# Sigmoid attention and an MLP mixer on one core: which unit transposes which tile, and a bias given as a number

## The chip, the cores and the metric

One core of a Trainium2 chip runs the whole program. The metric is the device time of one execution in microseconds (us), as the median of several runs. Kernels that are compared were run on the same chip in the same session. A ratio of two kernels is the mean time of one kernel's fast runs over the mean time of the other's fast runs of the same rounds, with a 95% interval, so it is not quite the ratio of the medians quoted beside it. Where I turn a ratio into microseconds, I multiply one minus the ratio by the median of the kernel before in that session.

TensorE is called PE in the profile (PEld is its weight load), VectorE DVE, ScalarE ACT, GpSimd POOL and SyncE SP. SP only issues DMA transfers here. The granted clock is the share of its full clock that PE was allowed at a time: 1.00 is full speed, 0.50 half.

## The reference, cut to what matters

```python
def _attn_ref(q, k, v):                       # 8 batches, 12 heads, 448 tokens, 64 wide
    scores = scale * q @ k.T - np.log(S)      # scale = 1/8, S = 448
    attn = 1.0 / (1.0 + np.exp(-scores))      # a sigmoid, no sum over a row
    return attn @ v

def _moe_ref(x, w_tok1, w_tok2, w_ch1, w_ch2):
    xt = x.transpose(0, 2, 1)                 # x: 8 x 448 x 768
    h = np.maximum(xt @ w_tok1, 0.0) @ w_tok2
    u = x + h.transpose(0, 2, 1)              # the "sums"
    h2 = np.maximum(u @ w_ch1, 0.0) @ w_ch2
    return u + h2
```

## The kernel before

The eight batches are four groups of two. A group has six head pairs, and each pair goes through scores (seven tiles `qk`, each followed by one sigmoid on ACT) and values. Then come the token mixing (`k` and `yn` in the profile), the sums u, and the channel mixing: 12 units of ch1 over token tiles 0 to 3, 12 over tiles 4 to 6, and 14 halves of ch2. While the channel mixing of one group runs (a "phase"), the attention of the next group is woven between its units, three rounds at a time. So group 0's attention stands alone at the start, and three mixed phases and one lone channel mixing follow.

Three things have to be transposed: k and q of each pair, the attention's result, and the sums. Cuts are marked `# ...`.

```python
def turn(n, whats=("k", "q")):                # k and q of head pair n (six per group)
    for what in whats:
        # ...
        if n >= NP:                           # groups 1 to 3: permute on DVE, transpose by DMA
            perm = pa.tile([128, J, 2, E], FP16, tag="perm", bufs=3, ...)
            nc.vector.tensor_copy(out=perm..., in_=raw[:, :, :, :])
            nc.sync.dma_start_transpose(out=t..., in_=perm...)
            continue
        ps = bank(f"t{what}_{n}", [128, J, 2, P], FP16)   # group 0: 14 transposes on PE; two PSUM buffers
        # ...
        nc.vector.tensor_copy(out=t[:, :, :, :], in_=ps[:, :, :, :])

def scores(self, i, j):                       # four matmuls into PSUM, then
    nc.scalar.activation(out=at[:, :, :], in_=ps[:, :, 0:S], func=SIGMOID,
                         bias=bias_t[:, :], scale=att_scale)     # bias_t: a [128, 1] tile

def attention_round(grp, r):
    # ...
    if j == 3 and not grp.first:              # two pairs ahead
        turn(grp.g * NP + i + 2)
    grp.scores(i, j)

def uturn(self, j, d0=0, d1=6, eng=nc.scalar, nj=1):      # the sums, by PE, emptied by ACT
    # ... nc.tensor.transpose per 128x128 block, then one copy out of PSUM

# end of a phase: what goes behind the halves of ch2
fronts = {
    0: lambda: front1(0),
    2: lambda: front1(1),
    3: lambda: front2((0, 1)),
    4: lambda: front2((2, 3)),
    5: lambda: (nxt.uturn(0, nj=2), front2((4, 5))),
    6: lambda: (nxt.uturn(2, nj=2), front2((6,))),
    7: lambda: nxt.uturn(4, nj=2),
}
```

## Time and profile before

| What | Before |
|---|---|
| median of 4 runs (lowest to highest) | 404.81 us (403.67 to 406.28) |
| span of the profiled run, PE busy in it | 401.5 us, 371.5 us |
| longest wait of PE, at group 1's first score tile | 7.5 us |
| first channel matmul of group 0 to the fifth channel unit | 67.54 to 85.77 us: 18.23 us |
| first channel matmul of group 2 to that of group 3 | 254.51 to 342.18 us: 87.67 us |
| one sigmoid of 128x896 | 1007 ns |

The two stretches in the table are the yardsticks of the whole study. The first contains the wait and the slow clock after it. The second is one complete mixed phase with one boundary between groups. The prediction shows the waits, the windows and the timeline behind them. From the page, only two lines are added: the first row of busy time and the granted clock in 40 slices of 10 us each.

```profile
PE 371.5 (93%) x3474; PEld 196.9 (49%) x3474; DVE 170.1 (42%) x315; ACT 203.4 (51%) x218; POOL 93.3 (23%) x159
...
PEclk9999999779999999999999999999999999999999
```

The two digits 7 lie between 70 and 90 us. ACT is busy for half the span, which reads like an engine that cannot matter. That reading is tested below.

### The profile page before, as it was taken

The page shows a single profiled execution, that of the slowest core. Times are in us where ns is not written, and L with a number is a line of the kernel's source. Part 1 is how long each engine was busy: PE and PEld are TensorE (multiplying, and loading weights), DVE is VectorE, ACT ScalarE, POOL GpSimd, SP SyncE. Part 2 cuts the span into 40 slices and gives each one's busy share as a digit, 9 for nine tenths or more (in the row PEclk, how much of TensorE's full clock was granted, in tenths as well). Part 3 has the DMA queues.
Part 4 walks back from the last instruction along what each step waited for, and adds up shares of the span by engine and source line. Part 5 has one row for each costly group of instructions (what it writes and reads, how often), then busy time and mean ns, then how long its engine had stood idle before and what let it go on. Part 6 is the DMA issues. An engine that isn't in the chain of part 4 may idle for free.

```text
span 401.5 us, 8197 instructions
## 1 busy us (share of the span) xinstructions
PE 371.5 (93%) x3474; PEld 196.9 (49%) x3474; DVE 170.1 (42%) x315; ACT 203.4 (51%) x218; POOL 93.3 (23%) x159
## 2 busy tenths in 40 slices
PE   2888877299999999999999999999999999999995
PEld 1444545134555555544555556544555556546663
DVE  1358686134432218644341229444431148455222
ACT  1996842168777531487867521687768312200000
POOL 9788171633333300033343200000000000000000
PEclk9999999779999999999999999999999999999999
DMA  7999999999999961179999952125433221000122
GB/s 107 183 176 165 204 190 205 142 133 150 157 135 159 211 138 61 59 71 166 154 127 149 229 96 79 41 46 72 93 59 112 64 80 41 39 0 2 78 102 95
DMA packets 79284, 45.85 MB, mean 114 GB/s; under 512 B 53008, under 2 KB 75536, under 8 KB 79248
## 3 DMA queue, kind: packets, MB, share of 16 engines
q0 software_dynamic: 25104, 21.93, 39.9%
q1 hardware_dynamic: 54144, 23.41, 31.4%
q8 instruction: 27, 0.44, 0.5%
q14 instruction: 9, 0.07, 0.1%
HBM read 43.84 MB, written 11.01 MB: 137 GB/s over the span
## 4 chain that ended last, share of the span: by engine, by line
PE 83%; DMA 9%; POOL 4%; DVE 2%; issue 1%; POOLq 0%; DVEq 0%
DMA k_3_1236<-in_k_dram 3%; DMA qT_1232<-qp_1233 2%; DMA w_tok_s<-in_moe_w_tok_dram 2%; DMA k_2_95<-in_k_dram 1%; DMA k_5_353<-in_k_dram 1%; PE c_0_2_0_1315 L321 1%; PE c_0_3_0_1323 L321 1%; PE c_2_4_1_4591 L338 1%; PE c_2_2_1_4421 L338 1%; PE c_2_2_0_4393 L338 1%; PE c_2_1_1_4332 L338 1%; PE c_2_0_1_4261 L338 1%; PE c_1_2_1_3290 L338 1%; PE c_1_2_0_3262 L338 1%; PE c_1_1_1_3184 L338 1%
## 5 line engine op out<-in xcount | busy, mean ns | idle before, releaser
L321 PEld LDWEIGHTS <-w_ch_t 128*128 128x128 f16 x576 | 53.9, 99 | 58.4 <-issue 14.3
L338 PEld LDWEIGHTS <-h2aT_1249 128*128 128x128 f16 x168 | 15.5, 98 | 13.2 <-issue 3.8
L338 PEld LDWEIGHTS <-h2aT_2460 128*128 128x128 f16 x168 | 15.4, 98 | 13.2 <-issue 3.8
L338 PEld LDWEIGHTS <-h2aT_3652 128*128 128x128 f16 x168 | 15.4, 98 | 13.2 <-issue 3.8
L338 PEld LDWEIGHTS <-h2aT_4783 128*128 128x128 f16 x168 | 16.4, 98 | 10.9
L211 PEld LDWEIGHTS <-w_tok_t 64*128 64x128 f16 x252 | 12.1, 94 | 9.4 <-issue 3.0
L239 PEld LDWEIGHTS <-w_tok_n 128*64 128x64 f16 x224 | 11.4, 109 | 9.6 <-issue 4.8
L91 POOL DMA_DIRECT2D k_0_2661<-in_k_dram x2 | 1.2, 604 | 38.9 <-DVE qp_2528 L111 38.9
L148 PE MATMUL qk_0_0_1277<-qT_1232,kT_1228 64*64 64x448 f16 x4 | 0.6, 566 | 7.5 <-DMA qT_1232<-qp_1233 7.5
L311 ACT ACTIVATE uT_3338<-ut_0_0_3548 128x1536 f16<-128x1536 f16 x1 | 1.5, 1451 | 8.9 <-PE ut_0_0_3548 L301 8.9
L311 ACT ACTIVATE uT_2146<-ut_0_0_2356 128x1536 f16<-128x1536 f16 x1 | 1.5, 1451 | 8.9 <-PE ut_0_0_2356 L301 8.9
L311 ACT ACTIVATE uT_4469<-ut_0_0_4679 128x1536 f16<-128x1536 f16 x1 | 1.4, 1450 | 8.9 <-PE ut_0_0_4679 L301 8.9
L122 PE MATMUL tk_135<-ident,k_0_77 128*64 128x128 f16 x14 | 1.0, 310 | 5.2 <-DMA k_0_77<-in_k_dram 5.2
L148 PEld LDWEIGHTS <-kT_1228 64*64 64x64 f16 x28 | 0.9, 123 | 8.9 <-issue 4.6
L155 ACT ACTIVATE attn_0_0_169<-qk_0_0_168,att_bias 128x896 f16<-128x896 f32 x1 | 1.0, 1007 | 7.5 <-PE qk_0_0_168 L148 7.5
L155 ACT ACTIVATE attn_0_0_1278<-qk_0_0_1277,att_bias 128x896 f16<-128x896 f32 x1 | 1.0, 1007 | 7.4 <-PE qk_0_0_1277 L148 7.4
L330 DVE TENSOR_SCALAR h2aT_1249<-c_0_2_0_1315 128x512 f16<-128x512 f32 x1 | 0.7, 692 | 7.1 <-PE c_0_2_0_1315 L321 7.1
L222 ACT ACTIVATE h1T_118<-k_0_0_512_1142 128x512 f16<-128x512 f32 x1 | 0.6, 597 | 5.4 <-PE k_0_0_512_1142 L211 5.4
L122 PEld LDWEIGHTS <-k_0_77 128*64 128x64 f16 x14 | 0.7, 164 | 5.1 <-DMA k_0_77<-in_k_dram 5.1
L222 ACT ACTIVATE h1T_3337<-k_2_0_384_3428 128x768 f16<-128x768 f32 x1 | 0.8, 810 | 4.7 <-PE k_2_0_384_3428 L211 4.7
L91 POOL DMA_DIRECT2D k_4_1306<-in_k_dram x2 | 1.3, 658 | 7.8 <-DVE qp_1233 L111 7.4
L222 ACT ACTIVATE h1T_2145<-k_1_0_384_2236 128x768 f16<-128x768 f32 x1 | 0.8, 811 | 4.4 <-PE k_1_0_384_2236 L211 4.4
(1293 smaller groups left out, 980.2 us busy)
## 6 DMA issues: line engine op xcount, KB each, us to landing
w_ch_t<-in_moe_w_ch_dram POOLq DMA_DIRECT2D x6, 768.0 KB, 11.2
w_tok_t<-in_moe_w_tok_dram POOLq DMA_DIRECT2D x2, 224.0 KB, 6.4
out_dram<-u_0_120 SPq DMA_DIRECT2D x1, 384.0 KB, 4.8
out_dram<-u_1_122 SPq DMA_DIRECT2D x1, 384.0 KB, 4.1
out_dram<-u_2_124 SPq DMA_DIRECT2D x1, 384.0 KB, 5.8
out_dram<-u_3_126 SPq DMA_DIRECT2D x1, 384.0 KB, 2.3
out_dram<-u_4_128 SPq DMA_DIRECT2D x1, 384.0 KB, 2.3
out_dram<-u_5_130 SPq DMA_DIRECT2D x1, 384.0 KB, 2.7
```

What stands on the lines that cost most here:

```text
L91: nc.gpsimd.dma_start(out=t[64 * b : 64 * b + 64, :, :, :], in_=src[2 * g + b, 2 * i : 2 * i + 2].rearrange("h (p j) e -> p h j e", j=J),)
L122: nc.tensor.transpose(out=ps[64 * h : 64 * h + 64, j, :, :], in_=raw[:, h, j, :], identity=ident[:, :],)
L148: nc.tensor.matmul(out=ps[64 * b : 64 * b + 64, h, 0:S], lhsT=kT[64 * h : 64 * h + 64, j, b, :], rhs=qT[64 * h : 64 * h + 64, :, b, :], st ...
L155: nc.scalar.activation(out=at[:, :, :], in_=ps[:, :, 0:S], func=SIGMOID, bias=bias_t[:, :], scale=att_scale,)
L211: nc.tensor.matmul(out=ps[:, b, 0 : c1 - c0], lhsT=w_tok1_t[64 * b : 64 * b + 64, j, 128 * tcb : 128 * tcb + 128], rhs=self.x_nat[64 * b : ...
L222: eng.activation(out=dst, in_=src, func=RELU)
L239: nc.tensor.matmul(out=d[64 * b : 64 * b + 64, :], lhsT=w_tok2_n[:, tcb, j, :], rhs=self.h1T[:, b, tcb, c0 + w * m : c0 + w * m + w], star ...
L311: eng.activation(out=dst, in_=src, func=COPYF)
L321: nc.tensor.matmul(out=ps[:, :, :], lhsT=w_ch1_t[:, db, 128 * cb : 128 * cb + 128], rhs=self.uT[:, db, j0:j1, :], start=(db == 0), stop=(d ...
L330: eng.tensor_scalar(out=dst, in0=ps[:, :, :], scalar1=0.0, scalar2=None, op0=MAX)
L338: nc.tensor.matmul(out=ps[:, :], lhsT=self.h2aT[:, cb, j, :], rhs=w_ch2_t[:, cb, c], start=(cb == 0), stop=(cb == NCB - 1),)
```

## The change

It has three parts. First, pairs 0 and 1 of group 1 are transposed by PE during group 0, which takes away the wait at group 1's first score tile. The last two of these evictions go to ACT. Second, the sigmoid's bias is an immediate number in place of a tile. Third, the sums of groups 1 to 3 are transposed by DMA, so that PE has 42 transposes fewer per group.

```diff
-    bias_t = pc.tile([128, 1], FP32, name="att_bias")
-    def turn(n, whats=("k", "q")):
+    def turn(n, whats=("k", "q"), eng=nc.vector):
-            if n >= NP:
+            if n >= NP + 2:
# ... the eviction goes to DVE or ACT as eng says
-                bias=bias_t[:, :],
+                bias=att_bias,
         def uturn(self, j, d0=0, d1=6, eng=nc.scalar, nj=1):
+            if not self.first:
+                for m in range(nj):
+                    nc.sync.dma_start_transpose(
+                        out=self.uT[:, :, j + m, :], in_=self.u16s[j + m][:, :]
+                    )
+                return
# first attention: pair 0 of group 1 is turned beside pair 5, pair 1 at the end
-        for i in range(NP - 1):
+        for i in range(NP):
             at(i, 1, turn, i + 1, "k")
             at(i, 3, turn, i + 1, "q")
# ... the x_nat transposes move with it
+        turn(NP + 1, "k", nc.scalar)
         grp.back(NP - 1)
+        turn(NP + 1, "q", nc.scalar)
# ... turn(NP) and turn(NP + 1) fall away at their old places
-            3: lambda: front2((0, 1)),
-            4: lambda: front2((2, 3)),
-            5: lambda: (nxt.uturn(0, nj=2), front2((4, 5))),
-            6: lambda: (nxt.uturn(2, nj=2), front2((6,))),
-            7: lambda: nxt.uturn(4, nj=2),
+            3: lambda: (front2((0, 1)), nxt.uturn(0, nj=2)),
+            4: lambda: (front2((2, 3)), nxt.uturn(2, nj=2)),
+            5: lambda: (front2((4, 5)), nxt.uturn(4, nj=2)),
+            6: lambda: (front2((6,)), nxt.uturn(6)),
# ... uturn(6) falls away at its old place, in the first channel unit of groups 1 to 3
-        nc.vector.memset(bias_t[:, :], att_bias)
```

More of the change, by code (lines that the diff above doesn't have):

```diff
@@ L126, in turn @@
                     )
-            nc.vector.tensor_copy(out=t[:, :, :, :], in_=ps[:, :, :, :])
+            if eng is nc.vector:
+                eng.tensor_copy(out=t[:, :, :, :], in_=ps[:, :, :, :])
+            else:
+                eng.activation(out=t[:, :, :, :], in_=ps[:, :, :, :], func=COPYF)
         if "q" in whats:
@@ L291, in uturn @@
         def uturn(self, j, d0=0, d1=6, eng=nc.scalar, nj=1):
+            if not self.first:
[4 more added lines that the diff above has]
+                return
             n = d1 - d0
             name = f"ut_{self.g}_{j}_{d0}"
-            if n == NDB:
-                ps = pp.tile([128, 2, 8, 128], FP16, tag="pair", bufs=3, name=name)
-            else:
-                ps = bank(name, [128, nj, n, 128], FP16)
+            ps = bank(name, [128, nj, n, 128], FP16)
             for m in range(nj):
@@ L379, in first_attention @@
         third = D // 3
-        for i in range(NP - 1):
+        for i in range(NP):
             at(i, 1, turn, i + 1, "k")
             at(i, 3, turn, i + 1, "q")
-            at(i + 1, 5, grp.back, i)
+            if i > 0:
+                at(i, 5, grp.back, i - 1)
         at(2, 5, permute_tok2)
@@ L415, in first_attention @@
         grp.tok2_late((6,), *cols)()
-        turn(NP)
         for f in late[1:]:
@@ L431, in unit @@
                     grp.uturn(6, 4, 6, nc.scalar)
-                if not grp.first and cb == 0:
-                    grp.uturn(6)
             units.append((1.3, unit))
@@ L456, in phase @@
         for t, f in units[:n_att]:
-            if grp.first and f is units[2][1]:
-                turn(NP + 1)
             f()
```

## The prediction

> **What bounds the kernel now.** I first read the page's share of busy time: TensorE (PE) is busy for 93% of the 401.5 us span and holds 83% of the chain that ended last, so PE's queue is the time, and only two things count: where PE stands still or runs slowly, and what PE does that another unit could do. The view of waits, for PE, gives the first at once:
>
> ```profile
> PE qk_0_0_1277 L148 <- DMA qT_1232<-qp_1233: 7.5, 1, 7.5
> PE tk_135 L122 <- DMA k_0_77<-in_k_dram: 5.2, 1, 5.2
> PE tq_152 L122 <- DMA q_0_80<-in_q_dram: 1.3, 1, 1.3
> ```
>
> Everything else PE waits for is under 1 us a time. The two lower rows are the start-up load, which the change leaves alone. The upper row is the first score matmul of group 1. The chain around it:
>
> ```profile
> 68.94 0.30 DVE qp_1233 L111
> ...
> 70.42 8.26 DMA qT_1232<-qp_1233
> ...
> 80.06 2.67 PE c_0_2_0_1315 L321 x6
> 82.73 2.42 PE c_0_3_0_1323 L321 x6
> 85.84 1.40 PE c_0_4_0_1369 L321 x6
> 87.24 1.29 PE c_0_5_0_1377 L321 x6
> ```
>
> VectorE (DVE) permutes q of the pair at 68.94 us, the DMA transpose needs 8.26 us, then PE starts again, and its first two groups of six channel matmuls need 2.67 and 2.42 us where the later ones need 1.29. So the wait is followed by slow work. The windows (PE busy, PEld, DVE, ACT, POOL, granted clock, DMA share, GB/s) show why:
>
> ```profile
> 65.00:79.00 14.00, 5.59 (x48) 2.88 (x46) 5.99 (x18) 3.15 (x6) 6.06 (x10) 0.84 1.34 161
> 79.00:85.00 6.00, 6.00 (x24) 1.84 (x16) 0.69 (x1) 2.80 (x3) 1.19 (x2) 0.51 1.38 153
> 85.00:119.00 34.00, 33.95 (x314) 16.11 (x314) 14.77 (x28) 27.43 (x30) 14.26 (x24) 1.00 1.13 144
> 141.00:167.00 26.00, 26.00 (x233) 15.31 (x228) 14.14 (x22) 6.40 (x7) 0.00 (x0) 1.00 0.31 82
> ```
>
> The clock is 0.51 just after the gap. From 85 us on PE is full: 33.95 of 34 us, 26.00 of 26 us. There only removing PE work helps. That work is seen in PE's timeline at the end of phase 0, where the sums of group 1 are transposed:
>
> ```profile
> 158.23 0.50 PE L301 MATMUL ut_0_0_2356<-ident,u_1_0_2148 128*128 128x128 f16 x6
> 158.57 0.50 PE L301 MATMUL ut_0_0_2356<-ident,u_1_1_2150 128*128 128x128 f16 x6
> 159.00 0.84 PE L239 MATMUL yn_4_0_2370<-h1T_2145,w_tok_n 128*64 128x384 f16 x8
> ...
> 165.88 0.50 PE L301 MATMUL ut_4_0_2446<-ident,u_1_4_2156 128*128 128x128 f16 x6
> 166.21 0.50 PE L301 MATMUL ut_4_0_2446<-ident,u_1_5_2158 128*128 128x128 f16 x6
> 166.55 1.46 PE L321 MATMUL c_1_0_0_2462<-uT_2146,w_ch_t 128*128 128x512 f16 x6
> ```
>
> Six transposes occupy PE for about 0.34 us (start to start), two tiles cost 0.67 to 0.77 with the switch.
>
> [...] Here one is 219 ns, and pipelined they start about 56 ns apart, so the spacing is what I count. [...] the sigmoid with the bias tile takes 1007 ns, the copy without one (xT of group 1) 918 ns, and a sigmoid behind that copy starts 0.81 us after it, against 0.89 behind another sigmoid. [...]
>
> **The change part by part.**
>
> *Pairs 0 and 1 of group 1 by TensorE.* Removed: four DVE permutes, four DMA transposes (SP), and with them the 7.48 us wait and the slow clock after it. Slow part: the two channel groups lose 1.38 and 1.13 us, the three score tiles before them start 0.33 to 0.37 us apart instead of 0.2, about 0.5 together. Removed from the path: 7.5 + 1.4 + 1.1 + 0.5 = 10.5 us; I take 10.3, since the first score tile now meets the two evictions in front of it.
> Added: 4 x 14 transposes on PE, 0.53 us per 14 (chain: tk_575 of pair 4), and four evictions, two on DVE (0.62 us each as kT of pair 4), two on ACT (about 0.9 us as xT). Where they lie, by the order of instructions: k of pair 0 stands in front of yn_0, which today waits 0.24 us for DVE: nearly free on PE. q of pair 0 stands where DVE is dense from 51.9 to 57.7 us and PE waits for it: 0.5 to 0.7. k and q of pair 1 enclose the last x_nat transpose; with two rotating PSUM buffers q must wait until ACT has emptied k, and the next token matmul comes about 0.8 us later. Sum: +1.5 us.
>
> *Bias immediate.* 168 sigmoids lose about 0.085 us of cadence, 14 us of ACT. But ACT bounds nothing after 30 us. Only from 13 to 28 us, PE waits 0.5 us at a time for sigmoids (14 of them there, 1.2 us). That is cut short by the load of pair 3: its k was issued at 14.77 us, needs 6.7 us, so it lands near 22.1, and the transpose that reads it already starts at 22.2. I count 0.7 us. The memset falls away beside the loads: nothing.
>
> *Sums of groups 1 to 3 by DMA.* Removed per group: 42 PE transposes, and four ACT evictions (3 x 1.45 + 0.81 us, off the path). PE: from the end of c_0_5_1 (158.40) to the end of c_1_1_0 (169.6) lie 11.2 us; the work that stays is 2 x 2.06 (ch2) + 2 x 1.3 (ch1) + 3 x 0.73 (token) = 8.9. So 2.3 us per group, which is 42 x 0.056: 6.9 us for three.
> Added: seven SP transposes per group. Are they in time? DVE finishes u16 of tiles 0 to 3 at about 153.8, 155.3, 157.3 and 158.7. SP needs 1.22 us to issue one; landing takes 2.9 us on a free DMA system (x_nat of group 3), and in 141 to 167 us the DMA share is 0.31 with no loads. The fourth tile lands near 158.8 + 2.9 = 161.7, say 162.2 behind the third. PE would reach the first ch1 at 166.55 - 2.0 = 164.6. Margin 2.4 us: hidden. Tiles 4 to 6 are wanted only 12 ch1 units later. DVE has 7 x 1.46 + 5 x 0.55 = 13 us of work in the now 13.1 us from 151.5 to 164.6: full, but not behind.
>
> Sum: -10.3 + 1.5 - 0.7 - 6.9 = -16.4 us.
>
> **The rivals.** (a) The wait comes back one pair later. With PE 10 us earlier, pair 2 (first to go through DMA now) is permuted near 75.5 us and wanted near 98.7 - 10.3 = 88.4. Its q landed 8.9 us after the issue before; near 77 + 8.9 = 86 now. For it: the DMA share is 1.34 there, and transposes took up to 13.5 us between loads. Against it: four transposes leave that very stretch, and k and q of pair 2 have landed since 56 us. If it happens, 2 to 4 us come back[...]: 391 to 394. (b) The DMA transposes of the sums come late: SP runs in order, and a store in front of tiles 4 to 6 waits for DVE, but tiles 0 to 3 have only a store that is ready at 152. A landing of 6 to 8 us, as under loads, would cost 2 to 3 us at three boundaries: about 396. The free DMA system there speaks against it. (c) The added transposes on PE and the two-buffer pool cost 3 us in place of 1.5: 390. (d) ACT gives more than I count, if the load of pair 3 comes earlier: 387.
>
> **Range and chances.** 404.6 - 16.4 = 388.2; I lean 0.6 us to the slow side for (a) and (b): 388.8 us. Eight in ten: 385.5 to 393.5, from all hits with the larger ACT gain up to one of (a) to (c) with 3 to 5 us. Two per cent is 8.1 us; to lose half of two independent gains (10.3 and 6.9) would take both rivals at once. Faster 0.97, same 0.025, slower 0.005.
>
> **What would show it.** Right: no PE wait over 1 us at the first score tile of group 1, a granted clock of 1.00 in the slices that were 7, PE full from about 67 us, sigmoid rows near 918 ns, seven SP transposes per group landing in about 3 us, 126 - 56 = 70 fewer matmuls (3474 to 3404), a span near 386. Wrong: PE waiting for qT of pair 2 or for uT at a boundary, a new dip of the clock, or PE gaps beside the new transposes adding over 3 us between 48 and 68 us.

## The result, and the profile after

The changed kernel took 386.95 us (median of 4 runs, 385.69 to 388.85) against 404.81 us, a ratio of 0.956 [0.951, 0.961]. The profiled run is the slowest of the four, at 388.85 us with a span of 387.1 us. It is used for places and mechanisms, and the medians for sizes.

| What | Before | After |
|---|---|---|
| first channel matmul of group 0 to the fifth channel unit | 18.23 us | 7.72 us |
| first token matmul of group 0 to the first channel matmul | 39.47 us | 43.06 us |
| first channel matmul of group 2 to that of group 3 | 87.67 us | 84.78 us |
| one sigmoid | 1007 ns | 917 ns |
| ACT busy | 203.4 us | 175.7 us |

First the page's two lines again, now of the kernel after:

```profile
PE 365.0 (94%) x3404; PEld 191.2 (49%) x3404; DVE 170.0 (44%) x312; ACT 175.7 (45%) x208; POOL 93.2 (24%) x159
...
PEclk9999998999999999999999999999999999999999
```

There are 70 matmuls fewer, as counted, and the two digits 7 are gone. A single 8 has appeared one slice earlier. The view of PE's waits after (engine, tile and line, what it waited for, total, times, longest) has no wait for a transposed q at the top any more:

```profile
PE tk_133 L121 <- DMA k_0_75<-in_k_dram: 5.1, 1, 5.1
PE tk_181 L121 <- DMA k_1_84<-in_k_dram: 1.5, 1, 1.5
...
PE yn_2_256_1054 L241 <- DVE qT_1024 L127: 0.8, 1, 0.8
...
PE tq_1201 L121 <- ACT kT_1174 L129: 0.5, 1, 0.5
```

The first two are the start-up load. The last two are new and belong to the added transposes: token mixing waits while DVE empties q of pair 0, and q of pair 1 waits until ACT has emptied k out of one of the two PSUM buffers. The chain of the kernel after, at the place where the prediction showed 8.26 us of DMA and then 2.67 and 2.42 us for the third and fourth channel unit, reads:

```profile
77.19 1.40 PE c_0_2_0_1365 L326 x6
78.59 1.29 PE c_0_3_0_1373 L326 x6
...
80.58 1.40 PE c_0_4_0_1419 L326 x6
```

The units after the score tiles now take what the later ones took before. The boundary of group 1 comes next, PE's timeline (start, length, line, tile, shape, count):

```profile
156.56 2.12 PE L343 MATMUL c_0_6_1_2460<-w_ch_t,h2aT_1316 128*128 128x384 f16 x12
158.52 1.46 PE L326 MATMUL c_1_0_0_2477<-uT_2196,w_ch_t 128*128 128x512 f16 x6
159.82 1.46 PE L326 MATMUL c_1_1_0_2485<-uT_2196,w_ch_t 128*128 128x512 f16 x6
```

No transpose stands between ch2 and ch1, and no wait does either. SP's timeline, and the last line of the view of the tile uT, say how near it was:

```profile
152.75 1.21 SPq L296 DMA_TRANSPOSE uT_2196<-u_1_3_2204  x1
```

```profile
DMA to landing us min/median/max: 2.7/2.7/3.2
```

The fourth tile was issued at 152.75 us, so it landed near 152.75 + 2.8 = 155.6 us, and PE wanted it at 158.52 us. That leaves a margin of 2.9 us.

The digit 8 is seen closer in the windows (PE busy, PEld, DVE, ACT, POOL, granted clock, DMA share, GB/s) of the kernel after:

```profile
62.00:64.00 2.00, 1.04 (x19) 0.67 (x19) 1.63 (x6) 0.00 (x0) 0.60 (x1) 1.00 1.15 210
64.00:66.00 2.00, 1.49 (x25) 1.25 (x25) 0.62 (x1) 0.92 (x1) 0.00 (x0) 0.73 1.16 208
66.00:68.00 2.00, 2.00 (x20) 1.39 (x22) 0.00 (x0) 1.27 (x2) 0.59 (x1) 0.50 1.17 214
```

The clock is at half from about 65 to 68 us, although the longest wait of PE before it was 0.84 us. This makes up 1.4 to 1.7 of the 3.6 us by which the stretch from the first token matmul to the first channel matmul grew (39.47 us before, 43.06 us after). It comes and goes between runs of the same kernel: in the profile of e0_whole the clock is 1.00 from 60 to 72 us.

### The profile page after: what moved, and what is told of

It is laid out like the page before. It is cut to its first block, busy times and chain, and to the rows that moved or that the text cites. A ratio compares the mean times of both kernels' runs of the same rounds, so it can differ in the third digit from the quotient of the medians.

```text
span 387.1 us, 8080 instructions
## 1 busy us (share of the span) xinstructions
PE 365.0 (94%) x3404; PEld 191.2 (49%) x3404; DVE 170.0 (44%) x312; ACT 175.7 (45%) x208; POOL 93.2 (24%) x159
## 4 chain that ended last, share of the span: by engine, by line
PE 87%; DMA 4%; DVE 4%; POOL 3%; ACT 1%; issue 1%; POOLq 0%
DMA k_3_106<-in_k_dram 2%; DMA q_1_87<-in_q_dram 2%; DMA k_5_351<-in_k_dram 1%; PE c_2_3_1_4494 L343 1%; PE c_2_3_0_4448 L343 1%; PE c_2_2_0_4357 L343 1%; PE c_2_1_1_4296 L343 1%; PE c_1_3_0_3360 L343 1%; PE c_1_2_0_3269 L343 1%; PE c_1_1_1_3191 L343 1%; PE c_0_3_0_2211 L343 1%; PE c_0_2_0_2120 L343 1%; PE c_0_1_1_2042 L343 1%; PE c_0_0_1_1971 L343 1%; PE c_2_6_1_4697 L343 1%; PE c_2_6_0_4671 L343 1%
## 5 line engine op out<-in xcount | busy, mean ns | idle before, releaser
L90 POOL DMA_DIRECT2D k_0_2668<-in_k_dram x2 | 1.2, 604 | 34.4 <-DVE kp_2531 L110 34.4
L157 ACT ACTIVATE attn_0_0_2494<-qk_0_0_2493 128x896 f16<-128x896 f32 x1 | 0.9, 917 | 17.4 <-PE qk_0_0_2493 L150 17.4
L157 ACT ACTIVATE attn_0_0_3643<-qk_0_0_3642 128x896 f16<-128x896 f32 x1 | 0.9, 917 | 17.4 <-PE qk_0_0_3642 L150 17.4
L157 ACT ACTIVATE attn_0_0_167<-qk_0_0_166 128x896 f16<-128x896 f32 x1 | 0.9, 917 | 7.5 <-PE qk_0_0_166 L150 7.5
L90 POOL DMA_DIRECT2D k_3_1955<-in_k_dram x2 | 1.2, 602 | 7.9 <-DVE qp_1808 L110 7.9
L90 POOL DMA_DIRECT2D k_3_3104<-in_k_dram x2 | 1.2, 602 | 7.9 <-DVE qp_2957 L110 7.9
L90 POOL DMA_DIRECT2D k_4_1217<-in_k_dram x2 | 1.2, 590 | 7.2 <-DMA w_ch_t<-in_moe_w_ch_dram 3.7
L224 ACT ACTIVATE h1T_2195<-k_1_0_384_2286 128x768 f16<-128x768 f32 x1 | 0.8, 811 | 4.4 <-PE k_1_0_384_2286 L213 4.4
L224 ACT ACTIVATE h1T_3344<-k_2_0_384_3435 128x768 f16<-128x768 f32 x1 | 0.8, 811 | 4.4 <-PE k_2_0_384_3435 L213 4.4
L224 ACT ACTIVATE h1T_4432<-k_3_0_384_4523 128x768 f16<-128x768 f32 x1 | 0.8, 811 | 4.4 <-PE k_3_0_384_4523 L213 4.4
L90 POOL DMA_DIRECT2D k_2_860<-in_k_dram x2 | 1.2, 590 | 6.8 <-PE xb_3_883 L196 3.5
L129 ACT ACTIVATE kT_1174<-tk_1175 128x896 f16<-128x896 f16 x1 | 0.9, 917 | 3.9 <-PE tk_1175 L121 3.9
```

Source lines behind the costliest of these rows:

```text
L90: nc.gpsimd.dma_start(out=t[64 * b : 64 * b + 64, :, :, :], in_=src[2 * g + b, 2 * i : 2 * i + 2].rearrange("h (p j) e -> p h j e", j=J),)
L129: eng.activation(out=t[:, :, :, :], in_=ps[:, :, :, :], func=COPYF)
L224: eng.activation(out=dst, in_=src, func=RELU)
```

## The experiments

"The whole" means the changed kernel. Twelve runs were made, e0_whole to e11_early, and all gave correct results. Each was taken beside the kernel before on one chip, but the sessions lie on different chips, so a comparison across sessions is less certain than one within a session.

**Together and apart (e0_whole, e1_pairs, e2_bias, e3_sums).** The first is the changed kernel once more, in the session of its three parts. Each of the others takes over the hunks of one part alone:

```diff
# e1_pairs: turn(), first_attention(), and the two dropped turn() calls
# e2_bias:  -bias=bias_t[:, :]  +bias=att_bias, memset and tile dropped
# e3_sums:  uturn() and fronts
```

> The changed kernel once more. In its first profile the work up to the first channel matmul of phase 0 (c_0_0_0) began at 72.79 us against 67.54 before, 5.25 us later, of which 1.5 us was a wait for the load of k of pair 1 at the start, and the clock was 0.50 from 66 to 68 us. Theory J (jitter of the start-up load): here the wait for that load is absent, c_0_0_0 begins at 70 to 71 us and the span is 385 to 386 us. Theory K (the change itself delays the start): c_0_0_0 again begins near 72.8 us. If the slow clock near 66 us belongs to the change, it is there again; if it was chance, it is not.

> Only the two pairs of group 1 by TensorE. The prediction's terms: gap and slow clock -10.3, added transposes +1.5, so 8.8 us shorter (about 396). What the first profile of the whole change suggests instead: the gap -10.5, but the added transposes +2.9 and a slow clock behind them +1.2, so about 6.4 us shorter (about 398.3).

> Only the immediate bias. The prediction: 0.7 us shorter, all of it before 30 us, nothing in the dense phases. Rival: the dense phases gain as well, since score tiles wait for PSUM that ACT empties 0.09 us sooner; from the whole change's profile the stretches between the boundaries are 0.5 to 0.85 us shorter than the removed transposes explain, so 2 to 3 us over three phases, and 2.5 to 3.5 us in all.

> Only the sums of groups 1 to 3 by DMA. The prediction: 2.3 us per boundary, 6.9 us in all, the DMA transposes landing about 3 us after their issue and no PE wait at the three boundaries. Rival: the whole difference between the boundaries (3.1, 3.2 and 2.9 us) comes from this part, 9.2 us. If the sum of the three parts' gains equals that of the whole change, they do not act on one another.

| Kernel | median us | runs | ratio [95%] | difference |
|---|---|---|---|---|
| before, same session | 404.47 | 27 | | |
| e0_whole | 388.44 | 6 | 0.9597 [0.955, 0.9645] | -16.3 |
| e1_pairs | 397.82 | 6 | 0.9824 [0.9778, 0.9869] | -7.1 |
| e2_bias | 401.91 | 22 | 0.994 [0.9918, 0.9961] | -2.4 |
| e3_sums | 397.23 | 6 | 0.9841 [0.979, 0.9891] | -6.4 |

The three differences add up to -15.9 us, the whole is -16.3. So the parts are independent as far as intervals of about 1 to 2 us either way can tell. The bias gives about three times what was predicted (1.6 to 3.3 us by its interval). The yardstick of a full phase, 87.67 us before, is 85.31 us in e3_sums (-2.36), 87.13 us in e2_bias (-0.54) and 84.78 us in e0_whole (-2.89): here, too, the parts add up. The start is the other place of the bias: the first token matmul stands at 27.32 us in e2_bias and at 28.07 us before, 0.75 us earlier, which is the size that the prediction had for all of it. This is one profile each, and the same place differs by up to 3.5 us between the profiles of this study, so these 0.75 us are not secured.

e0_whole was to decide between two theories of the late start in the first profile, and fits neither wholly. Its first channel matmul stands at 71.44 us and its span is 386.3 us. The start-up loads were late again (first token matmul at 30.04 us), but the stretch behind them took 41.40 us instead of 43.06, and the slow clock near 66 us was not there.

e3_sums found one thing that the whole hides. PE's waits in it contain this line:

```profile
PE k L211 <- DMA x_nat<-xT: 1.9, 2, 1.4
```

PE reaches the boundary earlier than before and waits up to 1.4 us for the transposed attention result of the last pair. In e0_whole this wait does not occur. The 1.4 us fall into the phase before the yardstick (87.97 us before), where the parts therefore do not add up: e2_bias saves 0.30 us there, e3_sums 1.15 and e0_whole 3.08.

**Only the slow clock taken away (e4_fill).** Is the cost of the gap its 7.5 us, or also the half clock after it? The kernel before gets 34 useless matmuls in the gap, which keep PE busy without moving any transfer.

```diff
             f()
+            if grp.first and f is units[1][1]:
+                ps = pair_bank("fill")
+                for m in range(34):
+                    nc.tensor.matmul(out=ps[:, m % 2, :], lhsT=ident[:, :],
+                                     rhs=w_ch1_t[:, 0, 0:512], start=True, stop=True)
```

> The kernel before, with 34 matmuls without use (128x512, about 7.4 us) put where TensorE waits for the transpose of q of pair 0 of group 1. Theory (the 10.5 us that the pairs part removes are two things, a wait of 7.5 us and about 3 us of half clock after it): the clock stays at 1.00, the first score matmul still starts about 11 us after c_0_0_0, the two channel groups behind it take 1.3 us each in place of 2.67 and 2.42, and c_0_4_0 starts about 15.2 us after c_0_0_0 in place of 18.2: 3 us shorter, about 401.5. Rival (the slow matmuls come from something else at that place, such as the DMA load): they stay slow and the time stays at 404.5.

Median 403.55 us of 20 runs against 404.04, ratio 0.9988 [0.9965, 1.0011]: the same. PE's timeline of e4_fill, and its window behind the gap, show that the edit did what it should:

```profile
72.12 7.50 PE L463 MATMUL fill<-w_ch_t,ident 128*128 128x512 f16 x34
...
80.25 2.76 PE L321 MATMUL c<-uT,w_ch_t 128*128 128x512 f16 x12
...
87.85 0.57 PE L148 MATMUL qk<-qT,kT 64*64 64x448 f16 x8 [1.14 <-ACT attn L155]
```

```profile
79.00:85.00 6.00, 6.00 (x46) 2.38 (x45) 2.08 (x4) 4.37 (x5) 1.43 (x4) 1.00 1.35 160
```

The clock is 1.00 where it was 0.51, and two channel units take 2.76 us. The first yardstick shrinks from 18.23 to 15.06 us, by 3.2 us, so the part of the half clock is confirmed. But the end does not come earlier by as much. A new wait of 1.14 us stands at the first score tile of pair 1. The view names ACT, but the trace has q of that pair issued at 77.11 us and landing 10.6 us later, at 87.72 us, and PE starts at 87.85 us: it waited for q. In the kernel before, that q was issued at 75.65 us and took 13.1 us, until 88.73 us, and PE came for it at 88.87 us. It was only just in time because PE had been slow. The stretch from the fifth unit to ch2 is then 34.31 us instead of 33.18, the profiled run began 1.04 us later, and the next phase loses another 0.6 us (88.60 us instead of 87.97), with a wait of 0.5 us for another q. This is a small lesson on additive accounts: a slow stretch can hide the next late transfer.

**Only one pair moved (e10_one).** If pair 1 is next in line, moving pair 0 alone should not pay.

```diff
# against e1_pairs
-            if n >= NP + 2:
+            if n >= NP + 1:
# turn(NP + 1) goes back to its old place in the first phase
```

> The kernel before, with only pair 0 of group 1 by TensorE; pair 1 stays with DMA as before. In the kernel before, q of pair 1 landed at 88.75 us and its first score matmul started at 88.87, so pair 1 was only just in time although TensorE had lost 10 us. With that loss gone TensorE should reach pair 1 near 80 us, and if its transposes take 5 to 9 us from an issue near 75 to 77 us it waits 1 to 5 us for them: the gain of the pairs part shrinks from about 7 us to 3 to 6 us (399 to 401). Rival: pair 1 lands sooner once two transposes are gone, no wait, and the gain is that of both pairs plus the 1 us of work saved (396.5).

Median 401.65 us of 9 runs against 404.96, ratio 0.9926 [0.9901, 0.995], or -3.0 us where both pairs give -7.1. PE's timeline of e10_one:

```profile
82.11 0.57 PE L151 MATMUL qk<-qT,kT 64*64 64x448 f16 x8 [2.35 <-DMA qT<-qp]
...
104.38 0.59 PE L151 MATMUL qk<-qT,kT 64*64 64x448 f16 x4 [4.19 <-DMA qT<-qp]
```

The q that PE waited for, tiles of 128x896, took 8.8 us (pair 1) and 11.3 us (pair 3) from issue to landing among the loads, where a 128x768 tile took 2.7 to 3.2 us at the boundary of the kernel after. Together with a third wait of 0.65 us, PE waits 7.2 us for later pairs, and behind the 4.19 us the clock was at 0.50 from 102.1 to 108.9 us. The 7.5 us wait has not gone, it has been spread, and the slow clock has moved with it. So the prediction's term for the gap is right for two pairs and would have been wrong for one.

**The sigmoid made longer (e5_pointer).** The claim under test is the prediction's "ACT bounds nothing after 30 us". The kernel before gets its scale as a second tile.

```diff
-                scale=att_scale,
+                scale=scale_t[:, :],     # a [128, 1] tile set by a memset
```

> The kernel before, with the scale of the sigmoid as a second per-partition pointer, so that each sigmoid takes about 0.09 us longer (1.10 us): the opposite of the immediate bias, twice removed from it. If the sigmoid's length reaches TensorE through PSUM in the dense phases, the stretch from the start of one phase to the next is 0.3 to 0.6 us longer in each, and the start longer by 0.7 to 1.5 us: 2 to 3 us in all, about 407. If ACT bounds nothing after 30 us (the prediction), the stretches of the dense phases stay the same to 0.1 us and only the start is longer.

The sigmoid takes 1098 ns, 91 ns more, about as much as the immediate bias takes off (1007 to 919 ns in e2_bias). Median 408.46 us, ratio 1.0102 [1.006, 1.0145], or +4.1 us. The full phase takes 88.49 us instead of 87.67. PE's waits after 100 us, where the kernel before has none for ACT, show in e5_pointer:

```profile
PE qk L149 <- ACT attn L156: 1.8, 6, 0.3
```

Score tiles wait for sigmoids in the dense phases. In the kernel before they do so too, too briefly for the view of waits. A round is three score tiles in a row. Three lines of the timeline before (one of ACT, two of PE), then PE's line of e2_bias for the same round, show it:

```profile
115.62 1.01 ACT L155 ACTIVATE attn_3_5_1785<-qk_3_5_1784,att_bias 128x896 f16<-128x896 f32 x1
...
116.29 0.36 PE L148 MATMUL qk_4_0_1814<-qT_1603,kT_1599 64*64 64x448 f16 x4
116.68 0.38 PE L148 MATMUL qk_4_1_1821<-qT_1603,kT_1599 64*64 64x448 f16 x4
```

```profile
116.32 0.76 PE L147 MATMUL qk<-qT,kT 64*64 64x448 f16 x12
```

Score tiles share three PSUM buffers (`bufs=3` in the code) with values and token mixing, so tile `qk_4_1` takes the buffer of `qk_3_5`, three tiles earlier. The sigmoid that empties it ends at 115.62 + 1.01 = 116.63 us, and the tile starts at 116.68 us, 0.39 us after the one before it, where 0.2 us is usual. By the trace's semaphores that sigmoid released it. With the shorter sigmoid the delay is gone. Two rounds stand 2.75 us apart there (113.33 and 116.08 us), and sigmoids in a row start 0.89 to 0.91 us apart before, 0.80 to 0.81 in e2_bias and 0.98 to 1.00 in e5_pointer, so three of them need about 2.7, 2.4 and 3.0 us. In each of the three mixed phases, three rounds are shorter in e2_bias, by 0.07, 0.22 and 0.22 us, which makes 0.5 us per phase and 1.6 us in all. In each phase of e5_pointer four rounds are longer, by 0.8 us together. ACT's mean load does not matter there, only its speed within a burst. In the second phase e2_bias keeps only 0.30 us, because PE loses 0.24 us again before the token mixing. With the 0.75 us of the start, that is 2.1 of the 2.4 us.

**The sums asked for later (e6_late, e8_order).** How much room does the third part have? e6_late issues each pair of the sums' transposes one half of ch2 later. e8_order swaps two pairs, so that tiles 2 and 3 stand behind 4 and 5.

```diff
# e6_late
-            3: lambda: (front2((0, 1)), nxt.uturn(0, nj=2)),
-            4: lambda: (front2((2, 3)), nxt.uturn(2, nj=2)),
+            3: lambda: front2((0, 1)),
+            4: lambda: (front2((2, 3)), nxt.uturn(0, nj=2)),
+            5: lambda: (front2((4, 5)), nxt.uturn(2, nj=2)),
# ... and so on to 7
# e8_order
-            4: lambda: (front2((2, 3)), nxt.uturn(2, nj=2)),
-            5: lambda: (front2((4, 5)), nxt.uturn(4, nj=2)),
+            4: lambda: front2((2, 3)),
+            5: lambda: (front2((4, 5)), nxt.uturn(4, nj=2), nxt.uturn(2, nj=2)),
```

> The whole change, with the DMA transposes of the sums one unit of work later, so that those of tiles 2 and 3 stand behind the store of tile 5 and issue about 3 us later. In the whole change the fourth landed 2.9 us before TensorE reached the first channel matmul of the next phase. If that is the margin, TensorE now waits between 0 and 1 us for uT at each of the three boundaries, and the time is 0 to 3 us longer than the whole change's. If the margin is much larger than it looks, nothing changes; if SP's order costs more than its issue times, waits of 2 us or more appear.

> The whole change, with the DMA transposes of tiles 2 and 3 issued behind those of tiles 4 and 5, which wait for DVE. By the whole change's trace the transpose of tile 3 is then issued near 158.7 us in its time scale and lands 2.7 us later at 161.4, where TensorE reaches the first channel matmul of the next phase at 158.5. If landing against arrival is the rule, TensorE waits 2.5 to 3.5 us for uT at each of the three boundaries, and 8 to 10 us are lost (about 396), more if the granted clock falls. If something else limits the boundary, less than half of that.

e6_late: 388.38 us (4 fast runs), ratio 0.9592 [0.9541, 0.9644], the same as the whole. There the fourth tile was issued at 151.77 us and landed at 154.62 us, and PE came for it at 155.39 us, so 0.8 us was left. e8_order: 402.03 us, ratio 0.9933 [0.9896, 0.9971], nearly all of the change's gain lost. PE waited at all three boundaries, 3.19, 3.19 and 3.10 us. PE's timeline at two of them:

```profile
159.34 2.75 PE L326 MATMUL c<-uT,w_ch_t 128*128 128x512 f16 x12 [3.19 <-DMA uT<-u]
```

```profile
247.47 5.28 PE L326 MATMUL c<-uT,w_ch_t 128*128 128x512 f16 x12 [3.19 <-DMA uT<-u]
```

The same wait of 3.19 us left the clock alone at the first boundary (2.75 us for 12 matmuls) and halved it at the second (5.28 us). The waits make 9.5 us, and the slow clock behind two of the three adds to them (at the third boundary, 28 matmuls took 7.89 us, where 12 took 2.75 at the first). The loss is about 13 us (402.03 against 388.44, with 0.5 us between the two sessions' medians of the kernel before). So the gain of the third part rests on the order of issue: SP issued the five transposes in program order, in a row from 152.23 to 158.89 us, with tiles 2 and 3 behind 4 and 5, where the kernel after issued tile 3 at 152.75 us. Tiles 0 to 3 must be asked for first.

**The added transposes made cheaper (e7_shadow, e9_keep).** In e7_shadow, ACT instead of DVE empties q of pair 0, and k and q of pair 1 stand where PE waits anyway. e9_keep is e7_shadow with four useless matmuls (0.9 us) in the 0.84 us wait near 59 us, to see whether work there prevents the chance slow clock.

```diff
# e7_shadow, against the whole
-            at(i, 3, turn, i + 1, "q")
+            at(i, 3, turn, i + 1, "q", nc.scalar if i == NP - 1 else nc.vector)
-        turn(NP + 1, "k", nc.scalar)
         grp.back(NP - 1)
-        turn(NP + 1, "q", nc.scalar)
+        turn(NP + 1, "k", nc.scalar)
# ... and turn(NP + 1, "q", nc.scalar) behind the second tok1
# e9_keep, against e7_shadow
+                for m in range(4):
+                    nc.tensor.matmul(out=keep[:, m % 2, :], lhsT=ident[:, :], ...)
```

> The whole change, with q of pair 0 emptied by ACT instead of DVE, and the transposes of pair 1 moved into TensorE's waits: k behind the last x_nat transpose, q behind the second token matmul, where TensorE waits for DVE. If the added 2 us of the pairs part are those waits (DVE dense at q of pair 0, two PSUM buffers at pair 1), the stretch from the first token matmul to c_0_0_0 shrinks from 41.4 us to about 39.6, and the time by about 2 us to 385. If the added cost is TensorE's own work of 4 x 0.53 us, it shrinks by under 0.5 us.

> The kernel with the transposes of pair 1 in the shadow of waits, and four matmuls without use (0.9 us) put where TensorE waits 0.84 us for DVE near 59 us. If the slow clock from 62 to 65 us comes from TensorE's low activity around 60 us, it is gone, the stretch from the first token matmul (behind 28 us) to c_0_0_0 falls from 41.6 to about 39.8 us and the time is 1.5 to 2 us below that kernel's. If the slow clock is chance, it may be there in the one profile or not, and the median moves by less than 1 us.

e7_shadow: 385.83 us, ratio 0.955 [0.9497, 0.9602]. e9_keep: 385.63 us, ratio 0.9525 [0.9503, 0.9547], the lowest median of the study. The 1.5 to 2 us over e7_shadow that were expected are not secured: the two intervals, of two sessions, overlap. From the first token matmul to the first channel matmul e9_keep takes 40.39 us with a clock of 1.00 throughout, and so does e11_early, which has the same placing and a fast profile, with 40.21 us; e0_whole, also without slow clock there, takes 41.40. So the placing, with the useless matmuls, is worth about 1 us. In e7_shadow the clock did fall, from 62 to 65 us, and the stretch was 41.61 us. Two of its six runs, of which no profile was kept, took 390.37 and 395.30 us.

e9_keep's profiled run was its slowest, 392.4 us, and counts as slow, so nothing of its speed after that stretch is used. But it shows a rival of the prediction at work. PE's timeline:

```profile
101.36 0.59 PE L150 MATMUL qk<-qT,kT 64*64 64x448 f16 x4 [4.92 <-DMA qT<-qp]
101.88 5.62 PE L326 MATMUL c<-uT,w_ch_t 128*128 128x384 f16 x18
```

q of pair 3, issued at 89.34 us, came about 12 us later, PE waited 4.92 us, and the 18 channel matmuls behind it took 5.62 us where e0_whole needs 3.10. In e0_whole PE waited 0.24 us for a q after the start-up, all of it. So the transposes among loads are still only just in time, and now and then they are not.

**Transposes of later pairs asked for earlier (e11_early).** If those transposes are only just in time, ask for them three score tiles sooner.

```diff
# against e9_keep
-        if j == 3 and not grp.first:
+        if j == 0 and not grp.first:
```

> The kernel with the kept-busy TensorE (385.6 us median, whose one profile, of the slow state, lost 4.9 us to a late q of pair 3), with each pair's permute and DMA transposes asked for three score tiles earlier, at the first tile of a pair in place of the fourth. If the time lost now and then in phase 0 is the landing of q of pairs 2 and 3 against TensorE's arrival, no wait for qT over 0.1 us is left in the profile, the slow executions vanish, and the median is 384 to 385 us. If the DMA system is simply full there, asking earlier moves the wait to another transfer and the time stays at 385.6.

Median 392.78 us against 404.35, ratio 0.9697 [0.9656, 0.9737], slower than e9_keep by some 7 us if the ratios of the two sessions are compared. No wait for q is left among PE's long ones. DVE's timeline and PE's waits of e11_early show what took its place:

```profile
102.57 0.39 DVE L110 COPY qp<-q 128x896 f16<-128x896 f16 x1 [5.13 <-DMA kT<-kp]
```

```profile
PE c L326 <- DVE h2aT L335: 4.2, 1, 4.2
```

The permuted copies have three buffers (`bufs=3` of the tag `perm`). Asked for early, the copy on DVE waits 5.13 us until a DMA transpose has given one back, and behind it, in order, wait the evictions that PE needs. The wait has moved from a transfer to a buffer and through DVE back to PE, and the clock was at 0.50 from 101.4 to 108.2 us. Another 2.1 us of waiting stand in the token mixing of the same phase. More permute buffers were not tried.

**When does the clock fall without a long wait?** This happened in four of the fourteen profiles: after, e2_bias, e7_shadow and e8_order. In each, the last values matmuls of group 0 end (61.2, 57.5, 58.4 and 58.7 us), and only transposes, one small token group of 0.4 us and waits under 0.9 us follow. The clock falls 3.5 to 3.7 us later (64.9, 61.1, 62.0 and 62.3 us) and stays at half for about 3.4 us. The kernel before has 3.5 us of such work (58.3 to 61.83 us), and the pairs' transposes lengthen it: in e0_whole it lasts from 61.3 to 65.72 us, 4.4 us. But the length alone decides nothing: with the longer stretch the clock fell in two profiles of five (after and e8_order, not e0_whole, e1_pairs and e6_late), and with the shorter one in two of seven. It stayed at 1.00 in e9_keep and e11_early, which have ordinary matmuls inside. The short waits in the stretch add up to 1.4 to 2.0 us, and those matmuls also fill one of them, so whether the transposes or the short waits make the clock fall, no run shows.

## Why the prediction was right

The time (388.8 predicted; 386.95 and 388.44 measured in two sessions) and the direction were right, and the large steps were too. Two small terms were off, in opposite directions. That the total came within 0.4 us in the second session is therefore partly luck.

- **The gap, -10.3 us.** Right: the first yardstick went from 18.23 to 7.72 us, -10.5. What the account did not say is that this needs both pairs. e10_one and e4_fill show that pair 1's transposes were next in line.
- **Added transposes, +1.5 us.** Mis-sized. Token mixing to channel mixing grew by 1.9 us in e0_whole and 2.1 in e1_pairs. The step that failed is q of pair 0, "0.5 to 0.7": with pair 0 alone, e10_one, the stretch is 40.82 us against 39.47, +1.35, of which about 1.1 us belong to q (0.5 us of transposes and a wait of 0.81 us for DVE, less a wait of 0.34 us that falls away, and small shifts) and 0.2 us to k, while pair 1 adds the other 0.76 (41.58 in e1_pairs), near the 0.8 predicted. The chance slow clock, 1.4 to 1.7 us in some runs, was not in the account at all.
- **Bias, -0.7 us.** Mis-sized: -2.4 us. The early part may be there, with 0.75 us. The step that failed is "ACT bounds nothing after 30 us". The rounds of score tiles gained 0.5 us in each of the three mixed phases of e2_bias, and lost 0.8 us in each of e5_pointer, since a third tile waits for the sigmoid that empties its buffer. I had read "bounds" from ACT's share of busy time, in a stretch where its bursts count.
- **Sums, -6.9 us.** Right: -2.36 us for one boundary without other waits, against 2.3 predicted (one transpose on PE took 219 ns, but what counted was the spacing of 56 ns: 42 x 0.056 = 2.35 us), and -6.4 us for the part alone, which then still waited for x_nat. The margin was 2.9 us where 2.4 was predicted, and landing 2.7 us where 2.9 was.
- **Rival (a), the wait comes back one pair later.** Not in the median, but real: 4.92 us for pair 3 in one run of e9_keep, and in e10_one, where pair 1 went by DMA, 7.2 us in the profile and more than half of the gain in the median. **Rival (b), the sums land late.** Did not happen; e8_order shows what it would have cost, about 13 us rather than the "2 to 3 us at three boundaries", because the waits are 3.1 to 3.2 us and the clock fell after two of them. **Rival (c)** was half right through the 1.9 to 2.1 us, **rival (d)** was right in giving ACT more, but mostly through the phases; whether the start-up load gave any of it is not shown.

Put together from the measured terms (the second and fourth from profiles without slow clock there, the third from medians), -10.5 + 1.9 - 2.4 - 3 x 2.36 is -18.1 us. The two sessions gave -17.8 and -16.3. Chance slow clock and the start-up loads (the first token matmul stands anywhere from 27.2 to 30.7 us in the profiles of this study) are of the size of what remains; I did not split it further.

What stays open: what exactly makes the clock fall near 60 us, and whether e9_keep beats the whole (0.9525 [0.9503, 0.9547] against 0.9597 [0.955, 0.9645] and 0.9561 [0.9508, 0.9613], in other sessions).

## What to carry to other kernels

Before you count the removal of a wait as a gain, look up when the next transfer behind it lands; if it was only just in time, you must move that one too, as e4_fill and e10_one show. Move transposes off the bounding engine where the DMA system is free (a share of 0.31 from 141 to 167 us in the kernel before), and check the order of issue against the order of need, since one swap of two lines cost 13 us. An engine with half its time idle can still set the pace inside a burst, as ACT did here at 51% busy, so test it by making its instruction a little longer before you write that it bounds nothing.
